# Convolution and low-rank mixer on one core: band built on chip, U laid out by matmuls, first two groups transposed on PE, x loads in held-back quarters

## The chip, the cores and the metric

The kernel runs on one core of one Trainium2 chip. The metric is the device time of one execution in microseconds (us). All but three of the timed runs were in the fast state. The three slow ones are left out of the ratios; they are still in the medians, where they move nothing by more than 0.3 us. The runs were made on different chips (the kernel before took 394.65 us in the median on the first, 392.8 to 393.2 in the later sets), so ratios are taken within one set. A ratio is the mean time of one kernel's fast runs over the mean of the other's fast runs of the same rounds, so it isn't quite the ratio of the medians quoted beside it.

Engine names are as in the profile: PE multiplies matrices, PEld loads its weights, DVE is the vector engine, ACT the scalar engine, POOL the engine that also issues the x and weight loads, SP the engine that issues the transposes and the stores. "uT" is the transposed u, "L311" a line of the kernel.

## The reference, cut to what matters

```python
# B, S, D = 8, 4224, 192;  8 heads of 24 columns, 7 taps;  rank 32;  hidden width 768
w = softmax(weight)                                   # [8 heads, 7 taps]
y[b, s] = sum_k w[head, k] * xpad[b, s + k]           # causal convolution along s, per head
h = (y^T @ U) @ V                                     # U: 4224 x 32, V: 32 x 4224
u = y + h^T
out = u + relu(u @ w_ch1) @ w_ch2                     # 192 -> 768 -> 192
```

`h` of any row needs all rows of its batch: `y^T @ U` (called tt below) sums over s. So a batch must be loaded and convolved whole before its first row of u exists.

## The kernel before

The 264 tiles of 128 rows are taken in 33 groups of eight; 33 tiles make a batch. PE does everything: the convolution as a matmul with a band matrix, tt, `h`, the first layer (W1) and the second (w2). W1 needs u with its 192 columns on the partitions, so each group's u is transposed by a DMA.

The band goes through DRAM (the softmax and some lines cut):

```python
    g_dr = tc.dram_tile([HB, H, GW], BF16, name="g_dr")
    nc.sync.dma_start(out=g_dr[:], in_=g_sb[:])
    band = cst.tile([P, H, P], BF16, name="band")
    for hf in range(2):
        nc.sync.dma_start(out=band[HB * hf : HB * hf + HB, :, :],
            in_=bass.AP(g_dr.tensor, g_dr.offset + HB, [[H * GW - 1, HB], [GW, H], [1, P]]))
```

U comes in rows of 64 bytes, straight into the layout that tt wants:

```python
    U_sb = cst.tile([P, NT, R], BF16, name="U_sb")
    nc.gpsimd.dma_start(out=U_sb[:], in_=moe_U[:].rearrange("(j p) r -> p j r", p=P))
```

The main loop loads x in whole batches. There are two x buffers, and nothing else holds POOL back: once a buffer's last convolution is multiplied, POOL issues the six loads of the next batch in a row (`...` marks a cut).

```python
    for g in range(NG + 1):
        if g + 1 < NG:
            h_group(g + 1)            # h by matmul, u = y + h on DVE
            transp(g + 1)             # DMA transpose of u, issued by SP
        for b in loadq.get(g, []):
            x_tile(b)
            for ch in XCH:
                x_load(b, *ch)        # two DMAs each, three chunks
        if g < NG:
            w1(g)                     # 36 matmuls, 12 PSUM banks, relu on ACT (8) and DVE (4)
        for b, h in convq.get(g, []):
            conv(b, h, 0, NB1, "AA")
        ...                           # w2(g-1) in four parts; tt_mm, tt_split in the middle
        for b in tts:
            tt_sum(b)                 # after the last part of w2
```

## Time and profile before

| | |
|---|---|
| time, median of three runs | 394.76 us (394.54 to 394.97) |
| span of the profiled run | 393.3 us, mean granted clock 0.953 |
| busy: PE, DVE, ACT | 84%, 60%, 48% |
| start of the first W1 | 43.3 us |
| PE waiting for uT, in six places | 32.2 us |
| group without / with two heads of convolution, undisturbed (the two differ in more than the convolution, see the last point of the account) | 8.73 / 9.20 us |

The page of the profile first: the span in 40 slices of 9.8 us, each digit the share of a slice in tenths; PEclk is the granted clock in tenths.

```profile
PE   0070599969996999969996999959999999999995
PEclk9996599999999899989999899978999999999998
DMA  9999925993599456994599456992544574546524
```

PE is idle in the first slices and dips again in five (the 9th, 13th, 18th, 22nd and 27th), each time in the second of two slices in which DMA is full. Now the waits of PE (microseconds in total, times, longest):

```profile
PE ps L311 <- DMA uT<-u_sb: 32.2, 6, 12.8
PE ps L183 <- DMA band<-g_dr: 19.9, 2, 19.3
PE ps L256 <- DVE tt_sb L233: 4.0, 8, 0.6
```

And the chain of waits (start, duration, what), followed back from the end:

```profile
...
5.40 5.85 DMA g_dr<-g_sb
...
11.95 8.22 DMA band<-g_dr
...
32.37 10.81 DMA uT<-u_sb
43.31 7.01 PE ps L311 x36
...
116.81 11.30 DMA uT<-u_sb
128.16 5.56 PE ps L311 x36
...
```

The band's trip through DRAM holds PE until 20.2 us. A transpose that has a median of 4.1 us to landing takes 10.8 and 11.3 us here, and the W1 after it is slow: 7.01 and 5.56 us instead of the 4.05 of an undisturbed group, because the clock was 0.50 when it began (43.3 to 46.7 us and 128.2 to 131.0 us). The timeline of POOL shows what had been issued just before the second of them (start, duration, engine, line, operation, count):

```profile
109.55 0.75 POOL L76 DMA_DIRECT2D x_sb<-in_x_dram  x1 [0.28 <-issue]
...
113.29 0.75 POOL L81 DMA_DIRECT2D x_sb<-in_x_dram  x1
```

These are the first and last of six loads, a whole batch in one burst; the transpose at 116.81 runs into it.

### The profile page before, as it was taken

Reading aid. Unit: us, or ns where it says so; the run is one execution under the profiler, and the core shown is the slowest. Engines: PE = TensorE matmul, PEld = TensorE weight load, DVE = VectorE, ACT = ScalarE, POOL = GpSimd, SP = SyncE. Lnnn points to the kernel's source line nnn. Section 1 sums busy time; section 2 is a strip of 40 time slices with the busy share of each in tenths; the row PEclk is TensorE's granted clock in tenths of the full one; section 3 lists DMA queues with packets and bytes.
Section 4 is the critical chain, followed back from the end, with each engine's and each line's share of the span. In section 5 each row is a group of like instructions: output and inputs, shape, how many; then the busy total and the mean of one; then the engine's idle time right before and its main releaser. Section 6 shows DMA issues by size and latency. Waiting matters only on the chain.

```text
span 393.3 us, 9471 instructions
## 1 busy us (share of the span) xinstructions
PE 330.9 (84%) x3956; PEld 221.1 (56%) x3956; DVE 236.6 (60%) x485; ACT 189.1 (48%) x410; POOL 46.2 (12%) x77
## 2 busy tenths in 40 slices
PE   0070599969996999969996999959999999999995
PEld 0060267646664577626664577626666676666674
DVE  2064176657766376647765376735766776778763
ACT  1050387526643556536643556515655664555440
POOL 8473002200040004000040003100000000000000
PEclk9996599999999899989999899978999999999998
DMA  9999925993599456994599456992544574546524
GB/s 120 179 170 188 123 44 124 205 201 93 128 148 192 112 130 118 215 176 95 131 149 170 117 136 120 202 189 63 132 110 115 130 140 113 130 122 136 148 90 153
DMA packets 130044, 54.63 MB, mean 139 GB/s; under 512 B 95248, under 2 KB 129936, under 8 KB 130000
## 3 DMA queue, kind: packets, MB, share of 16 engines
q1 hardware_dynamic: 88864, 39.41, 44.6%
q0 software_dynamic: 41136, 14.60, 33.7%
q8 instruction: 31, 0.51, 0.5%
q14 instruction: 13, 0.11, 0.1%
HBM read 29.47 MB, written 26.15 MB: 141 GB/s over the span
## 4 chain that ended last, share of the span: by engine, by line
PE 71%; DMA 22%; DVE 3%; ACT 1%; issue 0%; SPq 0%; DVEq 0%
PE ps L311 34%; PE ps L333 28%; DMA uT<-u_sb 17%; PE ps L183 5%; DMA band<-g_dr 2%; PE ps L256 2%; PE ps L210 2%; DMA g_dr<-g_sb 1%; DVE out_sb L341 1%; ACT y_sb L196 1%; DMA out_dram<-out_sb 1%; DMA w_sb<-in_weight_dram 1%; DVE tt_sb L233 1%; DVE u_sb L278 0%; DVE g_sb L142 0%
## 5 line engine op out<-in xcount | busy, mean ns | idle before, releaser
L321 ACT ACTIVATE rl_sb<-ps 128x512 bf16<-128x512 f32 x264 | 134.8, 619 | 160.9 <-PE ps L311 129.8
L311 PE MATMUL ps<-uT,W_sb 64*128 64x512 bf16 x1188 | 148.9, 398 | 32.3 <-DMA uT<-u_sb 32.2
L333 PE MATMUL ps<-W_sb,rl_sb 128*128 128x192 bf16 x1584 | 137.5, 246 | 0.0
L333 PEld LDWEIGHTS <-rl_sb 128*128 128x128 bf16 x1584 | 128.7, 98 | 12.1 <-issue 12.1
L311 PEld LDWEIGHTS <-W_sb 64*128 64x128 bf16 x1188 | 63.5, 98 | 107.8 <-issue 34.7
L341 DVE TENSOR_TENSOR out_sb<-ps,u_sb 128x384 f32<-128x384 f32 x132 | 73.5, 558 | 78.2 <-PE ps L333 77.1
L323 DVE TENSOR_SCALAR rl_sb<-ps 128x512 bf16<-128x512 f32 x132 | 88.3, 690 | 48.2 <-PE ps L311 48.1
L278 DVE TENSOR_TENSOR u_sb<-y_sb,ps 128x192 bf16<-128x192 bf16 (+1 forms) x168 | 66.3, 461 | 0.6 <-PE ps L256 0.6
L196 ACT ACTIVATE y_sb<-ps 128x384 bf16<-128x384 f32 (+3 forms) x136 | 53.5, 516 | 18.7 <-PE ps L183 18.5
L183 PE MATMUL ps<-x_sb,band 64*64 64x408 bf16 (+4 forms) x640 | 30.6, 319 | 20.0 <-DMA band<-g_dr 19.9
L183 PEld LDWEIGHTS <-band 64*64 64x64 bf16 x640 | 17.0, 116 | 34.1 <-DMA band<-g_dr 20.1
L72 POOL MEMSET x_sb<- 64x96 uint32 x8 | 1.4, 172 | 191.5 <-issue 155.9
L81 POOL DMA_DIRECT2D x_sb<-in_x_dram x24 | 18.8, 785 | 0.4
L76 POOL DMA_DIRECT2D x_sb<-in_x_dram x24 | 18.1, 754 | 1.8 <-issue 1.8
L256 PE MATMUL ps<-tt_sb,V_sb 32*128 32x192 bf16 x264 | 13.2, 246 | 4.0 <-DVE tt_sb L233 4.0
L198 DVE CAST y_sb<-ps 128x144 bf16<-128x144 f32 (+1 forms) x24 | 5.7, 297 | 17.1 <-PE ps L183 17.1
L256 PEld LDWEIGHTS <-V_sb 32*128 32x128 bf16 x264 | 4.6, 92 | 10.3 <-issue 10.3
L210 PE MATMUL ps<-y_sb,U_sb 128*32 128x192 bf16 x264 | 8.1, 252 | 0.9 <-ACT y_sb L196 0.9
L223 ACT ACTIVATE tt_hi<-ps 128x192 bf16<-128x192 f32 x8 | 2.6, 331 | 10.2 <-PE ps L210 10.2
L210 PEld LDWEIGHTS <-U_sb 128*32 128x32 bf16 x264 | 5.9, 97 | 2.5 <-issue 2.3
L224 DVE TENSOR_TENSOR tt_lo<-ps,tt_hi 128x192 bf16<-128x192 f32 x8 | 2.9, 358 | 5.4 <-ACT tt_hi L223 5.4
L233 DVE CAST tt_sb<-ps 128x192 bf16<-128x192 f32 x8 | 2.8, 348 | 0.3 <-PE ps L231 0.3
(24 smaller groups left out, 18.9 us busy)
## 6 DMA issues: line engine op xcount, KB each, us to landing
out_dram<-out_sb SPq DMA_DIRECT2D x132, 192.0 KB, 2.0
x_sb<-in_x_dram POOLq DMA_DIRECT2D x24, 288.0 KB, 8.4
x_sb<-in_x_dram POOLq DMA_DIRECT2D x8, 312.0 KB, 6.8
x_sb<-in_x_dram POOLq DMA_DIRECT2D x8, 240.0 KB, 15.2
x_sb<-in_x_dram POOLq DMA_DIRECT2D x8, 192.0 KB, 13.3
W_sb<-in_moe_w_ch_dram POOLq DMA_DIRECT2D x3, 288.0 KB, 6.0
uT<-u_sb SPq DMA_TRANSPOSE x33, 4.1
U_sb<-in_moe_U_dram POOLq DMA_DIRECT2D x1, 264.0 KB, 11.1
```

Of the source, the lines that this page charges most:

```text
L76: nc.gpsimd.dma_start(out=xt[b][0:HB, 1 + i0 : 1 + e0, :], in_=x[b, i0 * HB : e0 * HB, :].rearrange("(j p) d -> p j d", p=HB),)
L81: nc.gpsimd.dma_start(out=xt[b][HB:P, s0 : i1 + 1, :], in_=x[b, (NB0 - 1 + s0) * HB : (NB0 + i1) * HB, :].rearrange("(j p) d -> p j d", p=HB),
L183: nc.tensor.matmul(out=pp[r][HB * c : HB * c + HB, 0 : nn[r] * GS], lhsT=band[HB * r : HB * r + HB, h, HB * halo : HB * halo + HB], rhs=xt ...
L196: nc.scalar.activation(out=o, in_=i, func=ACT.Copy)
L210: nc.tensor.matmul(out=ttp[b][32 * c : 32 * c + 32, 0:D], lhsT=U_sb[:, j, :], rhs=yt[b][:, j, :], start=(ttn[b] < 4), stop=(ttn[b] + 4 >= NT),
L256: nc.tensor.matmul(out=banks[pr][:, a * D : (a + 1) * D], lhsT=V_sb[32 * q : 32 * q + 32, (j // 8) * 2 + j % 2, :], rhs=ttb[b][32 * q : 32 ...
L278: nc.vector.tensor_tensor(out=u_group(g)[:, i : i + n, :, hf, :], in0=yt[b][:, run[0] : run[0] + n, :].rearrange("p n (c k) -> p n c k", c=3),
L311: nc.tensor.matmul(out=pp[hf][:], lhsT=W1_sb[HB * hf : HB * hf + HB, c, m * P : (m + 1) * P], rhs=uTt[g][HB * hf : HB * hf + HB, :, c, :], ...
L321: nc.scalar.activation(out=rl[:, m, hf, :], in_=pp[hf][:], func=ACT.Relu)
L323: nc.vector.tensor_scalar_max(out=rl[:, m, hf, :], in0=pp[hf][:], scalar1=0.0)
L333: nc.tensor.matmul(out=cps[:, a * D : (a + 1) * D], lhsT=rlt[g][:, m, hf, (i + a) * P : (i + a + 1) * P], rhs=W2_sb[:, m, :], start=(m == ...
L341: nc.vector.tensor_tensor(out=o[:].rearrange("p n (c k) -> p n c k", c=3), in0=cps[:, 0 : 2 * D].rearrange("p (n c k) -> p n c k", n=2, c= ...
```

## The change

Its intent has two halves. The start: make the band on chip with DVE and PE, load U in wide rows and let PE lay it out, and bring the first two groups to W1 without a DMA transpose, from PE transposes of y and a directly multiplied transposed h. The main loop: load x in quarters, one quarter a group, each held back until that group's W1 has been multiplied, so that the load doesn't meet a transpose; run the convolution one slot earlier; sum tt one part of w2 earlier. The diff, cut to its core:

```diff
-    xs = ctx.enter_context(tc.tile_pool(name="xs", bufs=2))      # ys likewise 2 -> 3
+    xs = ctx.enter_context(tc.tile_pool(name="xs", bufs=3))
 ...
-    nc.gpsimd.dma_start(out=U_sb[:], in_=moe_U[:].rearrange("(j p) r -> p j r", p=P))
+    nc.gpsimd.dma_start(out=Ur[:, 0:nfull, :], in_=U4[0 : nfull * P, :].rearrange("(k p) c -> p k c", p=P))
 ...  (loads of the second x half, V, W1, W2)
+    Eq = cst.tile([P, 4, P], BF16, name="Eq")                     # selector for the layout of U
+    nc.gpsimd.memset(Eq[:], 0.0)
+    for jj in range(4):
+        nc.gpsimd.affine_select(out=Eq[32 * jj : 32 * jj + 32, :, :], ...)
 ...
+    for _ in range(20):                                           # warm-up
+        nc.tensor.matmul(out=wps[:], lhsT=zz[:, 0:P], rhs=zz[:], start=True, stop=True)
 ...  (softmax, now on 128 partitions; g_dr and its DMAs are gone)
+    for hh in range(2):
+        bp = bank()
+        for d in range(KC):
+            pr = sml.tile([P, HQ, BW], BF16, name="pr", bufs=4)
+            nc.vector.scalar_tensor_tensor(out=pr[:], in0=dif..., scalar=float(d), in1=c_sb...,
+                                           op0=ALU.is_equal, op1=ALU.mult)
+            nc.tensor.matmul(out=bp[:, 0 : HQ * BW], lhsT=ident[:], rhs=pr[:], start=(d == 0), stop=(d == KC - 1))
+        nc.scalar.activation(out=band[:, HQ * hh : HQ * hh + HQ, 0:BW], in_=bp..., func=ACT.Copy)
 ...
-    slots = [G - 5 + k // 2 for k in range(H)]
+    slots = [G - 6 + k // 2 for k in range(H)]                    # b = 2: [3]*3 + [4]*3 + [5]*2
+    for k, ch in enumerate(QCH):                                  # four quarters
+        loadq.setdefault(max(0, slots[0] - 4 + k), []).append((b, ch))
 ...
     for k, (i0, i1) in enumerate(XCH):                            # now two halves of batch 0
         for h in range(H):
             conv(0, h, i0, i1, "AD")
+        if k == 0:
+            u_layout()                                            # 16 matmuls with Eq, 4 copies
+            yT[0] = yT_part(0)                                    # 24 PE transposes of y
         tt_mm(0, ...)
-    tt_split(0); tt_sum(0); h_group(0); transp(0)
+    yT[1] = yT_part(1); tt_sum(0); hT_part(0, yT[0]); hT_part(1, yT[1])
 ...
+            last = w1(g)                                          # the W1's last matmul
+        if g == 0:
+            h_group(0); h_group(1)                                # u of the first two groups, for the output
+        for b, ch in loadq.get(g, []):
+            for r in range(2):
+                held(x_half(b, r, *ch), last)                     # load waits for it
 ...
+            if k == 2:                                            # was: after the last w2
+                for b in tts: tt_sum(b)
```

More of the change, by code (lines that the diff above doesn't have):

```diff
@@ L45 @@
     cst = ctx.enter_context(tc.tile_pool(name="cst", bufs=1))
-    xs = ctx.enter_context(tc.tile_pool(name="xs", bufs=2))
-    ys = ctx.enter_context(tc.tile_pool(name="ys", bufs=2))
+    xs = ctx.enter_context(tc.tile_pool(name="xs", bufs=3))
+    ys = ctx.enter_context(tc.tile_pool(name="ys", bufs=3))
     us = ctx.enter_context(tc.tile_pool(name="us", bufs=5))
@@ L56, in bank @@
         return psp.tile([P, 512], F32, name="ps", tag="ps")
-    w_sb = cst.tile([HB, H, KC], F32, name="w_sb")
-    nc.sync.dma_start(out=w_sb[:], in_=weight[:].partition_broadcast(HB))
+    w_sb = cst.tile([P, H, KC], F32, name="w_sb")
+    nc.sync.dma_start(out=w_sb[:], in_=weight[:].partition_broadcast(P))
     xt = [None] * B
@@ L67 @@
     NB1 = S // HB - NB0
-    XCH = [(0, 12), (12, 24), (24, NB1)]
     def x_tile(b):
@@ L72, in x_tile, with x_half @@
         nc.gpsimd.memzero(xt[b][0:HB, 0, :])
-    def x_load(b, i0, i1):
-        e0 = min(i1, NB0)
-        nc.gpsimd.dma_start(
-            out=xt[b][0:HB, 1 + i0 : 1 + e0, :],
-            in_=x[b, i0 * HB : e0 * HB, :].rearrange("(j p) d -> p j d", p=HB),
-        )
+    def x_half(b, r, i0, i1):
+        if r == 0:
+            e0 = min(i1, NB0)
+            return nc.gpsimd.dma_start(
+                out=xt[b][0:HB, 1 + i0 : 1 + e0, :],
+                in_=x[b, i0 * HB : e0 * HB, :].rearrange("(j p) d -> p j d", p=HB),
+            )
         s0 = i0 if i0 == 0 else i0 + 1
-        nc.gpsimd.dma_start(
+        return nc.gpsimd.dma_start(
             out=xt[b][HB:P, s0 : i1 + 1, :],
@@ L86, in x_load @@
         )
+    XCH = [(0, 16), (16, NB1)]
     x_tile(0)
-    x_load(0, *XCH[0])
-    x_load(0, *XCH[1])
-    U_sb = cst.tile([P, NT, R], BF16, name="U_sb")
-    nc.gpsimd.dma_start(out=U_sb[:], in_=moe_U[:].rearrange("(j p) r -> p j r", p=P))
-    x_load(0, *XCH[2])
+    for r in range(2):
+        x_half(0, r, *XCH[0])
+    HW = KC - 1
+    BW = HB + HW
+    dif = cst.tile([P, BW], F32, name="dif")
+    for r in range(2):
+        nc.gpsimd.iota(
+            dif[HB * r : HB * r + HB, :],
+            pattern=[[1, BW]],
+            base=0,
+            channel_multiplier=-1,
+            allow_small_or_imprecise_dtypes=True,
+        )
+    NUB = (NT + 3) // 4
+    Ur = cst.tile([P, NUB, 4 * R], BF16, name="Ur")
+    U4 = moe_U[:].rearrange("(n a) r -> n (a r)", a=4)
+    nfull = NT // 4
+    nc.gpsimd.dma_start(
+        out=Ur[:, 0:nfull, :], in_=U4[0 : nfull * P, :].rearrange("(k p) c -> p k c", p=P)
+    )
+    nlast = NT * 32 - nfull * P
+    nc.gpsimd.dma_start(out=Ur[0:nlast, nfull, :], in_=U4[nfull * P :, :])
+    for r in range(2):
+        x_half(0, r, *XCH[1])
     NSL = (NT + 7) // 8 * 2
     V_sb = cst.tile([P, NSL, P], BF16, name="V_sb")
+    full = NT // 8
     for q in range(4):
-        full = NT // 8
         src = moe_V[:, 0 : full * 8 * P].rearrange("r (k q t) -> r k q t", q=4, t=2 * P)
@@ L110 @@
     )
+    V0_sb = cst.tile([32, 2 * GT * P], BF16, name="V0_sb")
+    nc.gpsimd.dma_start(out=V0_sb[:], in_=moe_V[:, 0 : 2 * GT * P])
     W1_sb = cst.tile([P, 3, M4], BF16, name="W1_sb")
@@ L118 @@
     nc.gpsimd.dma_start(out=W2_sb[:], in_=moe_w_ch2[:].rearrange("(m p) d -> p m d", p=P))
-    g_sb = cst.tile([HB, H, GW], BF16, name="g_sb")
-    nc.vector.memset(g_sb[:], 0.0)
-    wm = cst.tile([HB, H], F32, name="wm")
-    nc.vector.tensor_reduce(out=wm[:], in_=w_sb[:], axis=mybir.AxisListType.X, op=ALU.max)
-    d_sb = cst.tile([HB, H, KC], F32, name="d_sb")
-    nc.vector.tensor_tensor(
-        out=d_sb[:],
-        in0=w_sb[:],
-        in1=wm[:].unsqueeze(2).to_broadcast([HB, H, KC]),
-        op=ALU.subtract,
-    )
-    e_sb = cst.tile([HB, H, KC], F32, name="e_sb")
-    nc.scalar.activation(e_sb[:], d_sb[:], ACT.Exp)
-    s_sb = cst.tile([HB, H], F32, name="s_sb")
-    nc.vector.tensor_reduce(out=s_sb[:], in_=e_sb[:], axis=mybir.AxisListType.X, op=ALU.add)
-    s2_sb = cst.tile([HB, H], F32, name="s2_sb")
-    nc.vector.tensor_scalar_add(s2_sb[:], s_sb[:], 1e-9)
-    rs_sb = cst.tile([HB, H], F32, name="rs_sb")
-    nc.vector.reciprocal(rs_sb[:], s2_sb[:])
-    for d in range(KC):
-        nc.vector.tensor_tensor(
-            out=g_sb[:, :, HB + d],
-            in0=e_sb[:, :, KC - 1 - d],
-            in1=rs_sb[:],
-            op=ALU.mult,
-        )
-    g_dr = tc.dram_tile([HB, H, GW], BF16, name="g_dr")
-    nc.sync.dma_start(out=g_dr[:], in_=g_sb[:])
-    band = cst.tile([P, H, P], BF16, name="band")
-    for hf in range(2):
-        nc.sync.dma_start(
-            out=band[HB * hf : HB * hf + HB, :, :],
-            in_=bass.AP(g_dr.tensor, g_dr.offset + HB, [[H * GW - 1, HB], [GW, H], [1, P]]),
+    Eq = cst.tile([P, 4, P], BF16, name="Eq")
+    nc.gpsimd.memset(Eq[:], 0.0)
+    for jj in range(4):
+        nc.gpsimd.affine_select(
+            out=Eq[32 * jj : 32 * jj + 32, :, :],
+            in_=Eq[32 * jj : 32 * jj + 32, :, :],
+            compare_op=ALU.not_equal,
+            fill=1.0,
+            base=0,
+            pattern=[[-1, 4], [1, P]],
+            channel_multiplier=-4,
         )
@@ L169 @@
         )
+    zz = cst.tile([P, 512], BF16, name="zz")
+    nc.vector.memzero(zz[:])
+    ident = cst.tile([P, P], BF16, name="ident")
+    wps = bank()
+    for _ in range(20):
+        nc.tensor.matmul(out=wps[:], lhsT=zz[:, 0:P], rhs=zz[:], start=True, stop=True)
+    band = cst.tile([P, H, P], BF16, name="band")
+    nc.vector.memzero(band[:])
+    e_sb = cst.tile([P, H, KC], F32, name="e_sb")
+    mx_sb = cst.tile([P, H], F32, name="mx_sb")
+    nc.vector.tensor_reduce(out=mx_sb[:], in_=w_sb[:], axis=mybir.AxisListType.X, op=ALU.max)
@@ new lines @@
+    d_sb = cst.tile([P, H, KC], F32, name="d_sb")
+    nc.vector.tensor_tensor(
+        out=d_sb[:],
+        in0=w_sb[:],
+        in1=mx_sb[:].unsqueeze(2).to_broadcast([P, H, KC]),
+        op=ALU.subtract,
+    )
+    nc.scalar.activation(e_sb[:], d_sb[:], ACT.Exp)
+    nc.vector.memzero(ident[:])
+    for r in range(2):
+        nc.vector.tensor_scalar(
+            out=ident[HB * r : HB * r + HB, HB * r : HB * r + HB],
+            in0=dif[HB * r : HB * r + HB, 0:HB],
+            scalar1=0.0,
+            scalar2=None,
+            op0=ALU.is_equal,
+        )
@@ new lines @@
+    s_sb = cst.tile([P, H], F32, name="s_sb")
+    nc.vector.tensor_reduce(out=s_sb[:], in_=e_sb[:], axis=mybir.AxisListType.X, op=ALU.add)
+    s2_sb = cst.tile([P, H], F32, name="s2_sb")
+    nc.vector.tensor_scalar_add(s2_sb[:], s_sb[:], 1e-9)
+    rs_sb = cst.tile([P, H], F32, name="rs_sb")
+    nc.vector.reciprocal(rs_sb[:], s2_sb[:])
+    c_sb = cst.tile([P, H, KC], F32, name="c_sb")
+    nc.vector.tensor_tensor(
+        out=c_sb[:],
+        in0=e_sb[:],
+        in1=rs_sb[:].unsqueeze(2).to_broadcast([P, H, KC]),
+        op=ALU.mult,
+    )
@@ new lines @@
+    HQ = H // 2
+    for hh in range(2):
+        bp = bank()
+        for d in range(KC):
+            pr = sml.tile([P, HQ, BW], BF16, name="pr", bufs=4)
+            nc.vector.scalar_tensor_tensor(
+                out=pr[:],
+                in0=dif[:].unsqueeze(1).to_broadcast([P, HQ, BW]),
+                scalar=float(d),
+                in1=c_sb[:, HQ * hh : HQ * hh + HQ, KC - 1 - d : KC - d].to_broadcast(
+                    [P, HQ, BW]
+                ),
+                op0=ALU.is_equal,
+                op1=ALU.mult,
+            )
+            nc.tensor.matmul(
+                out=bp[:, 0 : HQ * BW],
+                lhsT=ident[:],
+                rhs=pr[:],
+                start=(d == 0),
+                stop=(d == KC - 1),
+            )
+        nc.scalar.activation(
+            out=band[:, HQ * hh : HQ * hh + HQ, 0:BW],
+            in_=bp[:, 0 : HQ * BW].rearrange("p (h t) -> p h t", h=HQ),
+            func=ACT.Copy,
+        )
@@ new lines, with u_layout @@
+    U_sb = cst.tile([P, NUB, 4, R], BF16, name="U_sb")
+    def u_layout():
+        up = [bank() for _ in range(4)]
+        nb = [nfull + (1 if 32 * jj < nlast else 0) for jj in range(4)]
+        for a in range(4):
+            for jj in range(4):
+                nc.tensor.matmul(
+                    out=up[jj][:, 0 : nb[jj] * R],
+                    lhsT=Eq[32 * jj : 32 * jj + 32, a, :],
+                    rhs=Ur[32 * jj : 32 * jj + 32, 0 : nb[jj], a * R : (a + 1) * R],
+                    start=(a == 0),
+                    stop=(a == 3),
+                    tile_position=(32 * jj, 0),
+                )
+        for jj in range(4):
+            o = U_sb[:, 0 : nb[jj], jj, :]
+            i = up[jj][:, 0 : nb[jj] * R].rearrange("p (k r) -> p k r", r=R)
+            if jj % 2 == 0:
+                nc.scalar.activation(out=o, in_=i, func=ACT.Copy)
+            else:
+                nc.vector.tensor_copy(out=o, in_=i)
@@ L198, in conv @@
                 nc.vector.tensor_copy(out=o, in_=i)
-    ttp = [None] * B
-    ttb = [None] * B
-    ttn = [0] * B
+    ttb = [[] for _ in range(B)]
     def tt_mm(b, js):
-        if ttp[b] is None:
-            ttp[b] = bank()
-        for j in js:
-            c = ttn[b] % 4
+        p = bank()
+        for n, j in enumerate(js):
+            c = n % 4
             nc.tensor.matmul(
-                out=ttp[b][32 * c : 32 * c + 32, 0:D],
-                lhsT=U_sb[:, j, :],
+                out=p[32 * c : 32 * c + 32, 0:D],
+                lhsT=U_sb[:, j // 4, j % 4, :],
                 rhs=yt[b][:, j, :],
-                start=(ttn[b] < 4),
-                stop=(ttn[b] + 4 >= NT),
+                start=(n < 4),
+                stop=(n + 4 >= len(js)),
                 tile_position=(0, 32 * c),
             )
-            ttn[b] += 1
-    def tt_split(b):
         hi = sml.tile([P, D], BF16, name="tt_hi")
         lo = sml.tile([P, D], BF16, name="tt_lo")
-        nc.scalar.activation(out=hi[:], in_=ttp[b][:, 0:D], func=ACT.Copy)
-        nc.vector.tensor_tensor(out=lo[:], in0=ttp[b][:, 0:D], in1=hi[:], op=ALU.subtract)
-        ttb[b] = (hi, lo)
+        nc.scalar.activation(out=hi[:], in_=p[:, 0:D], func=ACT.Copy)
+        nc.vector.tensor_tensor(out=lo[:], in0=p[:, 0:D], in1=hi[:], op=ALU.subtract)
+        ttb[b] += [hi, lo]
     def tt_sum(b):
-        hi, lo = ttb[b]
         p = bank()
-        nc.tensor.matmul(out=p[:, 0:D], lhsT=R4[:], rhs=hi[:], start=True, stop=False)
-        nc.tensor.matmul(out=p[:, 0:D], lhsT=R4[:], rhs=lo[:], start=False, stop=True)
+        for n, part in enumerate(ttb[b]):
+            nc.tensor.matmul(
+                out=p[:, 0:D],
+                lhsT=R4[:],
+                rhs=part[:],
+                start=(n == 0),
+                stop=(n + 1 == len(ttb[b])),
+            )
         t = sml.tile([P, D], BF16, name="tt_sb")
@@ L300, in transp, with yT_part, hT_part @@
         )
+    def yT_part(g):
+        yT = uts.tile([P, 4, 3, P], BF16, name="yT", bufs=2)
+        tp = [psp.tile([P, 1024], BF16, name="ps", tag="ps") for _ in range(2)]
+        for n in range(12):
+            i, c = n // 3, n % 3
+            for hf in range(2):
+                nc.tensor.matmul(
+                    out=tp[n // 6][HB * hf : HB * hf + HB, (n % 6) * P : (n % 6 + 1) * P],
+                    lhsT=yt[0][:, GT * g + 4 * hf + i, HB * c : HB * c + HB],
+                    rhs=ident[:],
+                    start=True,
+                    stop=True,
+                    is_transpose=True,
+                    tile_position=(0, HB * hf),
+                )
+        for k in range(2):
+            o = yT[:, 2 * k : 2 * k + 2, :, :].rearrange("p i c t -> p (i c t)")
+            if k == 0:
+                nc.scalar.activation(out=o, in_=tp[k][:, 0 : 6 * P], func=ACT.Copy)
+            else:
+                nc.vector.tensor_copy(out=o, in_=tp[k][:, 0 : 6 * P])
+        return yT
+    def hT_part(g, yT):
+        uTt[g] = uts.tile([P, 4, 3, P], BF16, name="uT")
+        for c in range(3):
+            p = bank()
+            for hf in range(2):
+                nc.tensor.matmul(
+                    out=p[HB * hf : HB * hf + HB, :],
+                    lhsT=ttb[0][0:32, HB * c : HB * c + HB],
+                    rhs=V0_sb[:, (2 * g + hf) * 4 * P : (2 * g + hf + 1) * 4 * P],
+                    start=True,
+                    stop=True,
+                    tile_position=(0, HB * hf),
+                )
+            nc.vector.tensor_tensor(
+                out=uTt[g][:, :, c, :],
+                in0=yT[:, :, c, :],
+                in1=p[:].rearrange("p (i t) -> p i t", i=4),
+                op=ALU.add,
+            )
     RELU = ["AA", "AD", "AA", "AD", "AD", "AD"]
@@ L310, in w1 @@
                 for hf in range(2):
-                    nc.tensor.matmul(
+                    last = nc.tensor.matmul(
                         out=pp[hf][:],
@@ L323, in w1 @@
                     nc.vector.tensor_scalar_max(out=rl[:, m, hf, :], in0=pp[hf][:], scalar1=0.0)
+        return last
     out_t = out.rearrange("b s d -> (b s) d").rearrange("(t p) d -> p t d", p=P)
@@ L351 @@
     ttq = {}
+    loadq = {}
+    QCH = [(0, 8), (8, 16), (16, 24), (24, NB1)]
     for b in range(1, B):
         G = (b * NT) // GT
-        slots = [1] * 4 + [2] * 4 if b == 1 else [G - 5 + k // 2 for k in range(H)]
+        if b == 1:
+            slots = [1] * 4 + [2] * 4
+        elif b == 2:
+            slots = [3] * 3 + [4] * 3 + [5] * 2
+        else:
+            slots = [G - 6 + k // 2 for k in range(H)]
         for h, s in zip(range(H), slots):
@@ L357, with held @@
         ttq.setdefault(G - 2, []).append(b)
-    loadq = {}
-    for b in range(2, B):
-        G = (b * NT) // GT
-        loadq.setdefault(max(1, G - 10), []).append(b)
-    for (i0, i1) in XCH:
+        if b > 1:
+            for k, ch in enumerate(QCH):
+                loadq.setdefault(max(0, slots[0] - 4 + k), []).append((b, ch))
+    def held(ins, after):
+        tc.add_manual_dep(
+            ins.ins,
+            after.ins.name,
+            mybir.DependencyInfo(mybir.DependencyClass.Sync, mybir.DependencyReason.DATA),
+            reason="load held back",
+        )
+    yT = [None, None]
+    for k, (i0, i1) in enumerate(XCH):
         for h in range(H):
             conv(0, h, i0, i1, "AD")
-        tt_mm(0, list(range(i0 // 2, min(i1, NB0) // 2)) + list(range((NB0 + i0) // 2, (NB0 + i1) // 2)))
-    tt_split(0)
+        if k == 0:
+            u_layout()
+            yT[0] = yT_part(0)
+        tt_mm(
+            0,
+            list(range(i0 // 2, min(i1, NB0) // 2))
+            + list(range((NB0 + i0) // 2, (NB0 + i1) // 2)),
+        )
+    yT[1] = yT_part(1)
     tt_sum(0)
-    h_group(0)
-    transp(0)
+    hT_part(0, yT[0])
+    hT_part(1, yT[1])
     x_tile(1)
-    for ch in XCH:
-        x_load(1, *ch)
+    for ch in QCH:
+        for r in range(2):
+            x_half(1, r, *ch)
     for g in range(NG + 1):
-        if g + 1 < NG:
+        if g + 1 < NG and g > 0:
             h_group(g + 1)
             transp(g + 1)
-        for b in loadq.get(g, []):
-            x_tile(b)
-            for ch in XCH:
-                x_load(b, *ch)
         if g < NG:
-            w1(g)
+            last = w1(g)
+        if g == 0:
+            h_group(0)
+            h_group(1)
+        for b, ch in loadq.get(g, []):
+            if ch[0] == 0:
+                x_tile(b)
+            for r in range(2):
+                held(x_half(b, r, *ch), last)
         for b, h in convq.get(g, []):
@@ L389 @@
         tts = ttq.get(g, [])
-        if g > 0:
-            w2(g - 1, 0)
-            w2(g - 1, 1)
-        for b in tts:
-            tt_mm(b, range(NT))
-            tt_split(b)
-        if g > 0:
-            w2(g - 1, 2)
-            w2(g - 1, 3)
-        for b in tts:
-            tt_sum(b)
+        for k in range(4):
+            if g > 0:
+                w2(g - 1, k)
+            if k == 1:
+                for b in tts:
+                    tt_mm(b, range(NT))
+            if k == 2:
+                for b in tts:
+                    tt_sum(b)
 _INS = ['x', 'weight', 'moe_U', 'moe_V', 'moe_w_ch1', 'moe_w_ch2']
```

## The prediction

> **What bounds the kernel now.** The span is 393.3 us. From 295.0 us on the chain of waits shows PE back to back, 8.73 us for a group without convolution (346.30 to 355.03), 9.2 with two heads, clock 1.0: bound by PE. 31 such groups, 56 heads at 0.405 us, seven U sums at 0.9, the lone first W1 (4.4) and the 16.7 us from the last W1's start to the end give about 321 us after the first W1 starts, at 43.3 us: 364. The other 29 us are lost in the middle.
>
> - PE's waits: 32.2 us for the transposed u, 12.8 at the start and 19.4 in five later places. There the chain shows 10.5 to 12.3 us for a transpose (median 4.1), and the timeline six x loads issued in a row just before (109.5 to 114.0 us), DMA share above 1.2 until 130. The Trainium skill, "DMA: Bandwidth & Descriptors", section "Issuing engines are not separate DMA queues", says all queues share 16 engines and interleave; this trace agrees.
> - After each such wait the clock falls to 0.50 and W1 takes 5.5 to 7.0 us instead of 4.05 ("TensorE: Matmul & The Clock Gate", Part 1, says idling halves the clock; the windows show it): about 10 us in all.
> - 4.0 us waiting for tt_sb, eight times 0.5.
>
> Start: PE waits until 19.3 us for the band (g_dr 5.85 us, band 8.2 us by DMA), although the last x chunk landed by 17.9 (waits of POOL). Then 8 us of convolution, tt and h, then the 10.8 us first transpose.
>
> **What the change does, costed.**
> - Band on chip: after the softmax (5.3 us) 14 vector operations of 280 elements at about 0.37 us (estimate from the 0.36 us of a 192-wide subtract): ready near 11.5 us, like the first x half. PE can start 8 us earlier.
> - U layout: 16 matmuls and four evictions, 1.5 to 2 us. But its selector Eq stands on POOL behind all weight loads, and POOL stalls until the load issued eight earlier has landed (as at 9.9, 12.3, 15.8 now). I expect Eq at 19 to 22 us, and PE, in order, idle from 14 until then. This returns much of the band's gain.
> - After Eq: layout, 24 transposes, tt, second convolution half, tt, 24 transposes, tt_sum, h transposed: about 12.5 us. First W1 near 33.5 us, warm, instead of 43.3 cold: 10 plus 3 us gained.
> - Given back: six adds of 128x512 (0.69 us) and twelve u additions (0.47) meet the relus on DVE in groups 0 and 1: 15 us of DVE against 10 of PE; PE stalls 3 to 4 us.
> - Held quarters: a transpose is issued 2 us into a group and lands 4 us later; a quarter of x starts only after W1, at 4.4 us. Nearly all 19.4 us of waits and 7 us of cold W1 go; 1 to 2 us remain.
> - tt_sum one w2 earlier: 3 to 4 us gained.
>
> **Sum.** 33.5 + 321 + 3.5 + residue 0 to 2 = 358 span; times lie 1.5 above it: 359 us. Range 351 to 368. Faster by over 2%: 0.95; within 2%: 0.04; slower: 0.01.
>
> **What would show it.** First W1 at 31 to 36 us; PE's wait for uT below 3 us; clock 1.0 from 40 us; u_layout preceded by a wait for Eq; 8.73 us groups unchanged; W1 of group 0 or 1 stretched by DVE.
>
> **What would make it wrong.** Eq much later or earlier; quarters landing on the transposes all the same, since 28 of 33 groups carry one; the transpose of group 2 held up by x(1) and x(2), leaving a cold stretch near 45 to 55 us.

## The result, and the profile after

The kernel after takes 354.05 us (353.87 to 354.23, four runs); before, 394.65 us. The ratio is 0.8984, with a 95% interval of 0.8945 to 0.9023: 10% faster. The span is 352.1 us, the mean clock 0.981, PE is busy 96% of it. The page's slices, now 8.8 us each:

```profile
PE   8589899999999999999999999999999999999995
PEclk9869899999999999999999999999999999999999
DMA  9979989976989899878969897899445454555535
```

From the sixth slice on PE has no dip left, and the load traffic is spread evenly instead of coming in bursts. The waits of PE:

```profile
PE ps L256 <- POOL Eq L151: 4.6, 4, 3.8
PE ps L356 <- DVE u_sb L378: 0.7, 3, 0.2
```

No wait for uT by DMA is left in the list; a transpose has a median of 3.7 and a maximum of 5.2 us to landing, against 4.1 and 12.7. A new wait stands first, for Eq. The chain of waits in the start:

```profile
...
15.73 0.89 POOL W_sb L145
...
20.03 1.03 PE ps L256 x10
...
30.96 2.36 PE ps L455 x20
33.35 1.99 DVE rl_sb L467 x3
35.34 2.79 DVE u_sb L378 x6
38.17 5.73 PE ps L455 x35
...
```

The first W1 runs at 30.0 us (its main part at 30.96) instead of 43.3. The second takes 5.73 us, as slow as one after a transpose wait: between 34.5 and 38.2 us PE was busy for 2.4 of 3.7 us, since it could only put in its h matmuls as DVE freed banks one by one. The busy time by stretch shows the clock there (stretch, PE, PEld, DVE, ACT and POOL busy with counts, clock, DMA share, GB/s):

```profile
36.00:38.00 2.00, 1.18 (x9) 0.47 (x8) 2.00 (x5) 0.00 (x0) 1.70 (x3) 1.00 0.93 100
40.00:42.00 2.00, 2.00 (x12) 0.89 (x10) 1.50 (x3) 1.12 (x3) 0.00 (x0) 0.54 1.23 140
```

Last, one quarter and the transposes around it, in the timelines of POOL and SP:

```profile
105.26 0.69 POOL L76 DMA_DIRECT2D x_sb<-in_x_dram  x1 [8.96 <-PE ps L455]
105.94 0.70 POOL L81 DMA_DIRECT2D x_sb<-in_x_dram  x1
```

```profile
103.12 1.43 SPq L397 DMA_TRANSPOSE uT<-u_sb  x1
...
112.32 2.71 SPq L397 DMA_TRANSPOSE uT<-u_sb  x1
```

POOL had waited 8.96 us for W1 (L455). The two loads of the quarter go out 2 us after one transpose and 6 us before the next, land 3.7 to 4.1 us later, and so fit between.

The undisturbed groups are what they were: in the chain W1, w2 and h of a group without convolution take 8.73 us (306.06 to 314.79).

### The profile page after: what moved, and what is told of

It reads as the page before. It is cut to its first block, busy times and chain, and to the rows that moved or that the text cites. A ratio compares the mean times of both kernels' runs of the same rounds, so it can differ in the third digit from the quotient of the medians.

```text
span 352.1 us, 9621 instructions
## 1 busy us (share of the span) xinstructions
PE 338.9 (96%) x4004; PEld 228.7 (65%) x4004; DVE 246.1 (70%) x500; ACT 191.0 (54%) x409; POOL 56.5 (16%) x98
## 4 chain that ended last, share of the span: by engine, by line
PE 90%; DVE 4%; DMA 3%; POOL 2%; issue 1%; ACT 0%; POOLq 0%
PE ps L455 39%; PE ps L478 38%; PE ps L284 6%; DMA x_sb<-in_x_dram 3%; PE ps L356 2%; PE ps L308 2%; DVE u_sb L378 1%; DVE y_sb L299 1%; PE ps L409 1%; POOL Eq L151 1%; DVE rl_sb L467 1%; DVE uT L439 1%; POOL x_sb L76 0%; PE ps L325 0%; DVE out_sb L486 0%
## 5 line engine op out<-in xcount | busy, mean ns | idle before, releaser
L465 ACT ACTIVATE rl_sb<-ps 128x512 bf16<-128x512 f32 x264 | 133.3, 623 | 121.5 <-issue 66.2
L455 PE MATMUL ps<-uT,W_sb 64*128 64x512 bf16 x1188 | 143.6, 380 | 0.8 <-DVE uT L439 0.2
L478 PEld LDWEIGHTS <-rl_sb 128*128 128x128 bf16 x1584 | 128.8, 98 | 12.2 <-issue 12.2
L455 PEld LDWEIGHTS <-W_sb 64*128 64x128 bf16 x1188 | 64.3, 95 | 69.2 <-issue 14.0
L297 ACT ACTIVATE y_sb<-ps 128x384 bf16<-128x384 f32 (+2 forms) x128 | 52.6, 528 | 0.3
L76 POOL DMA_DIRECT2D x_sb<-in_x_dram x30 | 21.2, 705 | 178.7 <-PE ps L455 163.2
L284 PE MATMUL ps<-x_sb,band 64*64 64x408 bf16 (+3 forms) x576 | 29.5, 335 | 0.0
L81 POOL DMA_DIRECT2D x_sb<-in_x_dram x30 | 22.1, 736 | 0.0
L180 PE MATMUL ps<-zz 128*128 128x512 bf16 x20 | 6.0, 471 | 1.2 <-DVE zz L176 1.2
L256 PE MATMUL ps<-Ur,Eq 32*128 32x256 bf16 (+1 forms) x16 | 2.2, 410 | 4.6 <-POOL Eq L151 4.6
L299 DVE CAST y_sb<-ps 128x192 bf16<-128x192 f32 (+1 forms) x16 | 5.1, 366 | 1.0 <-PE ps L284 1.0
```

The costliest lines, as they stand in the source:

```text
L76: return nc.gpsimd.dma_start(out=xt[b][0:HB, 1 + i0 : 1 + e0, :], in_=x[b, i0 * HB : e0 * HB, :].rearrange("(j p) d -> p j d", p=HB),)
L81: return nc.gpsimd.dma_start(out=xt[b][HB:P, s0 : i1 + 1, :], in_=x[b, (NB0 - 1 + s0) * HB : (NB0 + i1) * HB, :].rearrange("(j p) d -> p j ...
L284: nc.tensor.matmul(out=pp[r][HB * c : HB * c + HB, 0 : nn[r] * GS], lhsT=band[HB * r : HB * r + HB, h, HB * halo : HB * halo + HB], rhs=xt ...
L297: nc.scalar.activation(out=o, in_=i, func=ACT.Copy)
L455: last = nc.tensor.matmul(out=pp[hf][:], lhsT=W1_sb[HB * hf : HB * hf + HB, c, m * P : (m + 1) * P], rhs=uTt[g][HB * hf : HB * hf + HB, :, ...
L465: nc.scalar.activation(out=rl[:, m, hf, :], in_=pp[hf][:], func=ACT.Relu)
```

## The experiments

Twelve variants ran, all correct. "First W1" is its first matmul in the trace; "uT wait" is PE's total wait for DMA transposes.

| run | built on | time, us | ratio to before (95%) | first W1, us | uT wait, us |
|---|---|---|---|---|---|
| before | | 394.65 | 1 | 43.3 | 32.2 |
| after | | 354.05 | 0.8984 (0.8945 to 0.9023) | 30.0 | 0 |
| loads_only | before | 366.64 | 0.9324 (0.929 to 0.9359) | 36.3 | 9.9 |
| old_loads | after | 381.90 | 0.971 (0.9669 to 0.9752) | 30.1 | 18.2 |
| no_hold | after | 381.34 | 0.9713 (0.9646 to 0.978) | 30.3 | 16.7 |
| whole_held | after | 379.22 | 0.9645 (0.9602 to 0.9689) | 30.0 | 20.1 |
| eq_early | after | 349.58 | 0.8891 (0.8857 to 0.8925) | 26.1 | 0 |
| u_direct | after | 347.57 | 0.8855 (0.8825 to 0.8886) | 23.3 | 0 |
| band_dram | after | 355.81 | 0.9065 (0.9033 to 0.9097) | 31.7 | 0 |
| dma_first | after | 363.32 | 0.9237 (0.9193 to 0.928) | 38.8 | 12.3 |
| u_direct_band_dram | u_direct | 357.44 | 0.9088 (0.9036 to 0.9141) | 32.6 | 0 |
| u_direct_spread | u_direct | 351.03 | 0.8923 (0.8878 to 0.8968) | 23.3 | 2.8 |
| sum_late | after | 357.25 | 0.908 (0.9035 to 0.9124) | 30.1 | 0 |
| conv_back | after | 353.61 | 0.8999 (0.8952 to 0.9045) | 30.0 | 0 |

The kernel after was timed in an earlier set than its variants, so a difference of two medians in this table carries the 1 to 2 us by which sets differ; conv_back, which does the same work, came within 0.5 us of it in the last set. All the larger differences below also hold between the ratios, but their sizes shift: taken from the ratios, the gain of eq_early is 3.7 us (4.5 from the medians), that of u_direct 5.1 (6.5), the loss of band_dram 3.2 (1.8) and that of sum_late 3.8 (3.2). The spans of the profiled runs agree with the medians for u_direct (345.4 against 352.1) and band_dram (353.9). No run undoes the warm-up matmuls, the third y buffer or the two halves of batch 0 by themselves, and none tries the held quarters with two x buffers.

The first two questions are how the 40 us divide between the loads and the start, and what it is about the loads that helps: their size, their time, or the third buffer.

### loads_only: the loads of the change, nothing else

```diff
 (kernel before)
-    xs ... bufs=2
+    xs ... bufs=3
-        loadq.setdefault(max(1, G - 10), []).append(b)
+        for k, ch in enumerate(QCH):
+            loadq.setdefault(max(0, G - 9 + k), []).append((b, ch))
 ...
+            last = w1(g)
+        for b, ch in loadq.get(g, []):
+            for ld in x_load(b, *ch): held(ld, last)
```

> The kernel before, with only its x loads changed: four quarters per batch, one a group, each held until the first layer (W1) of its group has been multiplied. Theory: the five later waits for the transposed u (19.4 us) and the slow first layers after them (about 7 us) came from whole-batch loads, so both go, the start stays at 43.3 us, and the time is 366 to 370 us. Rival: the start-up work is most of the gain, and the later waits only move; then the time stays above 380 us.

Measured: 366.64 us. The time is inside the expected interval, but the way there isn't the expected one. The chain of waits:

```profile
32.09 4.05 DMA uT<-u_sb
36.28 4.37 PE ps L312 x24
...
44.53 11.50 DMA uT<-u_sb
56.08 4.01 PE ps L312 x19
```

The start did not stay at 43.3 us. The first transpose took 4.05 us instead of 10.81, although the loads of V, the weights and x(1) are there as before. What is missing is x(2): in the kernel before, its buffer became free when the last convolution of x(0) was multiplied, and its six loads went out just before the transpose.

```profile
27.85 0.17 POOL L72 MEMSET x_sb<- 64x96 uint32 x1 [1.80 <-PE ps L183]
...
32.07 0.72 POOL L81 DMA_DIRECT2D x_sb<-in_x_dram  x1
```

So about 7 us of the wait at the start were the same collision as the later ones. In return this run loses time at the transpose of group 2 (11.50 us): the first three quarters of x(2) were issued close together, from 42.2 to 48.0 us, in groups 0 and 1. PE waits 3.85 us there and its W1 is slow again (5.75 us), about 5.5 us in all.

### old_loads: everything but the loads

```diff
 (kernel after)
-    xs ... bufs=3
+    xs ... bufs=2
-            for k, ch in enumerate(QCH): loadq.setdefault(max(0, slots[0] - 4 + k), []).append((b, ch))
+            loadq.setdefault(max(1, G - 10), []).append(b)
-                held(x_half(b, r, *ch), last)            # after w1
+            for ch in [(0, 12), (12, 24), (24, NB1)]: ... x_half(b, r, *ch)     # before w1, not held
```

> The kernel after, with the loads of before put back (whole batches, not held, two x buffers). Theory: the start-up gain (13 us) and the early tt_sum (3 us) stay, the waits for transposes come back: 374 to 384 us, with some 4 us of waiting at each of about five places. Rival: with the start gone the transposes no longer collide; then under 360 us.

Measured: 381.90 us, PE waits 18.2 us for uT in five places, as before. The rival falls. The two runs agree on the division: the loads are worth 26 to 28 us (392.8 to 366.6 from one side, 381.9 to 354.05 from the other), the rest of the change 11 to 13 us. That they agree so well is partly luck: the 26 of loads_only include the 7 us at the start, which the change cures a second time by its new start, less the 5.5 us that this run loses anew at group 2.

### no_hold: quarters, but not held back

```diff
 (kernel after)
-                held(x_half(b, r, *ch), last)
+                x_half(b, r, *ch)
```

> The kernel after, with the quarters no longer held back; they start as soon as a buffer is free. Theory: it is the release after W1 that keeps a load off the next transpose; without it the eight pieces of a batch run in one burst and PE waits for transposes again: 370 to 384 us. Rival: cutting the loads in quarters (or the third buffer) is enough; then 354 to 357 us.

Measured: 381.34 us. POOL, held by nothing but a free buffer, issues all eight pieces of a batch in a row; here the last of them, and the piece of the chain of waits that follows:

```profile
101.01 0.80 POOL L81 DMA_DIRECT2D x_sb<-in_x_dram  x1
```

```profile
102.39 11.35 DMA uT<-u_sb
113.79 5.37 PE ps L455 x36
```

Quarters and a third buffer alone give back nothing of the 27 us. The rival falls.

### whole_held: held back, but a whole batch at once

```diff
 (kernel after)
-                loadq.setdefault(max(0, slots[0] - 4 + k), []).append((b, ch))
+                loadq.setdefault(max(0, slots[0] - 4), []).append((b, ch))
```

> The kernel after, with all four quarters of a batch released at one point, after the W1 of the first of the four groups. Theory: a batch takes 10 to 12 us, longer than the 4.7 us left of the group, so it runs into the next transpose and costs 3 to 5 us at each of six batches: 366 to 378 us. Rival: the point of release is what matters, not the size; then 354 to 357 us.

Measured: 379.22 us, a little above the expected interval; PE waits 20.1 us in six places. Held release alone gives next to nothing either (2.7 us less than old_loads, and the intervals of the two ratios overlap): the burst starts after W1 and is still running when the next transpose is issued. Of the kernels tried, only those with both, a load small enough and released at the right time, are free of the collision in the main loop.

### eq_early: the selector built before the weight loads

Now the start. PE's only large wait after the change is for Eq, which POOL builds behind the weight loads:

```profile
16.66 0.52 POOL L149 MEMSET Eq<- 128x512 bf16 x1
17.26 2.72 POOL L151 TENSOR_SCALAR_AFFINE_SELECT Eq<-Eq 32x512 bf16<-32x512 bf16 x4
```

```diff
 (kernel after: the block that builds Eq moved up)
     for r in range(2):
         x_half(0, r, *XCH[1])
+    Eq = ...; nc.gpsimd.memset(...); 4 x nc.gpsimd.affine_select(...)
     (loads of V, V0, W1, W2)
-    Eq = ...
```

> The kernel after, with the selector Eq built on POOL before the loads of V and the weights are issued, instead of behind them. Theory: PE's wait of 4.6 us for Eq goes, and the cold stretch from 14 to 22 us with it; the second x half landed by 15.1 us; the first W1 moves from 30.0 to 25 to 27 us and the time from 354.0 to 349 to 351 us. Rival: the weight loads, now issued 3 us later, or the second x half become the next wait; then under 2 us are gained.

Measured: 349.58 us, first W1 at 26.1 us, no wait for Eq: 4.5 us gained, as expected. A cost that nobody had expected shows up beside it. The operations that build the band, read by tile (shortest, median and longest in ns), first in the kernel after, then in this run:

```profile
L225 DVE SCALAR_TENSOR_TENSOR pr<-dif,c_sb x14: 440/442/451, 5.8 to 10.6; 128x280 bf16<-128x280 f32 x14
```

```profile
L225 DVE SCALAR_TENSOR_TENSOR pr<-dif,c_sb x14: 435/438/885, 7.3 to 13.7; 128x280 bf16<-128x280 f32 x14
```

While POOL makes its selections (7.4 to 10.6 us), a DVE operation takes up to 885 ns instead of 442, and a selection 734 instead of 630. The convolution starts at 14.5 instead of 11.4 us. About half of these 3 us is this slowing (the fourteen operations take 6.9 us from first to last instead of 5.2). The other half is a later beginning (7.25 instead of 5.81): DVE's wait for the convolution weights ended 0.8 us later in this profile (4.59 against 3.79), although nothing before that load was changed, and the small vector operations after it took 0.6 us longer. The Trainium skill states this in "GPSIMD Engine Reference", section "Specifications": POOL shares its SBUF interfaces with DVE, with contention for DVE instructions that have two SBUF inputs. `scalar_tensor_tensor` has two here, and this trace agrees.

### u_direct: U loaded as before, no layout

```diff
 (kernel after)
-    Ur ... two loads in rows of 256 bytes;  Eq ...;  u_layout()
+    U_sb = cst.tile([P, NT, R], BF16, name="U_sb")
+    nc.gpsimd.dma_start(out=U_sb[:], in_=moe_U[:].rearrange("(j p) r -> p j r", p=P))
```

> The kernel after, with U loaded straight into its layout as before (4224 packets of 64 bytes), without Eq and the layout matmuls. Theory: the old U load took about 3.6 us of the queue against about 1 us now, so the second x half lands near 18 us, where PE now waits for Eq until 20.0 and lays U out until 21; so the layout by matmuls gains nothing: 352 to 355 us. Rival: the old load also holds the whole queue up and the layout is worth its 2 us and more: over 356 us.

Measured: 347.57 us, 6.5 us faster than the kernel after and below the expected interval; the fastest kernel. The layout of U by matmuls doesn't merely gain nothing, it costs 6.5 us. Most of this is the wait for the selector: eq_early, which has the layout without that wait, stands only 2.0 us above u_direct in the same set. The first convolution half ends at 15.0 us and the transposes of y follow at once, where the kernel after does them at 21.0. The expectation erred in what the 64-byte load costs: the wait of POOL for the last part of the second x half ends at 16.27 us against 15.11, so it delays x by 1.2 us (it had been reckoned at 2.6, and x at 18 us):

```profile
15.11 0.63 POOL L140 DMA_DIRECT2D W_sb<-in_moe_w_ch_dram  x1 [1.75 <-DMA x_sb<-in_x_dram]
```

```profile
16.27 0.63 POOL L133 DMA_DIRECT2D W_sb<-in_moe_w_ch_dram  x1 [1.77 <-DMA x_sb<-in_x_dram]
```

In the kernel before, U had seemed to take 3.6 us of the queue (12.2 to 15.8). The band's DMAs ran in that time, but they are not the reason: u_direct_band_dram below has both, and there the wait ends at 16.33 us. More likely the 3.6 us were shared with the last two x loads, which landed 0.9 and 2.0 us after U (16.7 and 17.9 us); no run shows it.

### band_dram: the band through DRAM again

```diff
 (kernel after)
-    (14 x scalar_tensor_tensor and matmul with ident, 2 copies)
+    (g_sb on 64 partitions, g_dr, two band DMAs, as in the kernel before)
```

> The kernel after, with the band built through DRAM as before. Theory: the band comes near 19 us instead of 11.5; PE is in order, so the first convolution half (2.8 us) then stands after the wait instead of inside it, and since Eq holds PE until 20.0 anyway, only some 3 to 4 us of the 8 are lost, with the colder clock: 356.5 to 359 us. Rival: the full 8 us are lost: 361 us or more.

Measured: 355.81 us, first W1 at 31.7 us: 1.8 us lost, less than either theory had. PE waits for the band until 20.15 us, but Eq would have held it until 20.0 in any case, and the convolution then runs into a U layout that needs no wait.

### u_direct_band_dram: the same, with the selector out of the way

```diff
 (u_direct)
-    (band on chip)
+    (band through DRAM)
```

> The run u_direct (347.6 us) with the band through DRAM as well. Theory: in band_dram the loss was only 1.8 us because PE would have waited for Eq until 20.0 us anyway; with Eq gone nothing hides the band, which comes at about 20 us instead of 12.3, so about 8 us are lost: 354.5 to 357 us. Rival: the band through DRAM is cheap by itself; then 348 to 350.5 us.

Measured: 357.44 us, first W1 at 32.6 instead of 23.3 us. Without Eq in the way the band on chip is worth 9.9 us, with it 1.8. The two parts of the change stand in the way of each other: one takes a wait of PE away, the other puts a new one in the same place. Its runs spread wider than the others (355.27 to 359.14 us), so the 9.9 is uncertain by some 2 us; the time is also slightly above the expected interval.

### dma_first: the first two groups transposed by DMA

```diff
 (kernel after)
-            yT[0] = yT_part(0)
-    yT[1] = yT_part(1); tt_sum(0); hT_part(0, yT[0]); hT_part(1, yT[1])
+    tt_sum(0); h_group(0); transp(0)
-        if g + 1 < NG and g > 0:
+        if g + 1 < NG:
```

> The kernel after, with the first two groups transposed by DMA as before. Theory: the x(1) load runs beside the first transpose as it did before, so it takes 7 to 11 us, PE idles that long and goes cold, while the transposes on PE (2.4 us) and the second set of adds fall away: 361 to 366 us. Rival: the first transpose costs its 4 us of landing only: 355 to 358 us.

Measured: 363.32 us. The transpose of group 0 takes 7.86 us beside the load of x(1), and the one of group 2 takes 10.11:

```profile
30.84 7.86 DMA uT<-u_sb
...
47.55 10.11 DMA uT<-u_sb
```

The transposes on PE are worth 9.3 us here, the largest part of the new start. A rival to them was not tried: to release x(1) later and keep the DMA transposes. In loads_only, where x(1) was issued by 25.4 us, the first transpose at 32.09 took only 4.05 us.

### u_direct_spread: fewer u additions between the first two W1

```diff
 (u_direct)
-        if g == 0:
-            h_group(0)
-            h_group(1)
+        if g in (1, 2):
+            h_group(g - 1)
```

> The run u_direct with the u additions of groups 0 and 1 moved behind the W1 of groups 1 and 2, so that no more than eight of them stand in one group. Theory: PE's stall on banks between the first two W1 (27.9 to 31.0 us, where three groups of matmuls alone take about 1 us) and the cold second W1 (6.2 instead of 4.1 us) come from twelve additions in a row on DVE; both go: 343 to 345 us. Rival: the earlier transpose of group 2 then falls on the loads of x(1) and x(2) and PE waits for it: 347 us or more.

Measured: 351.03 us, 3.5 us slower than u_direct (2.7 from the ratios, whose intervals touch): the rival was right, although the theory's mechanism was there too. The stall between the first two W1 is gone and the second W1 is warm; but the transpose of group 2, issued at 30.49 instead of 34.22 us, now stands in the loads of x(1) and x(2), and lands only after 12.0 us:

```profile
28.23 4.10 PE L411 MATMUL ps<-uT,W_sb 64*128 64x512 bf16 x36
...
42.54 5.49 PE L411 MATMUL ps<-uT,W_sb 64*128 64x512 bf16 x36 [2.77 <-DMA uT<-u_sb]
```

The stall on DVE had been holding the transpose out of the burst. Whether a later release of the first quarters of x(2) would let both gains stand has not been tried.

### sum_late and conv_back: the two small parts

```diff
 (sum_late: kernel after)                          (conv_back: kernel after)
-            if k == 2: tt_sum                     -   slots = [3]*3 + [4]*3 + [5]*2   and  G - 6 + k // 2
+        (after the last w2): tt_sum               +   slots = G - 5 + k // 2           for b = 2 to 7
```

> The kernel after, with tt_sum behind the last w2 of its group, as before. Theory: PE waits 0.5 us for tt_sb at each of seven batches: 357 to 358 us. Rival: under 355 us.

Measured: 357.25 us, 3.2 us more, and the waits of PE show why:

```profile
PE ps L356 <- DVE tt_sb L333: 3.5, 7, 0.6
```

> The kernel after, with the convolutions of batches 2 to 7 one group later, as before (the loads follow them). Theory: the PE work is the same and y is needed only in the group with tt, where PE then waits 0.1 to 0.2 us for ACT; the time stays within 1 us of 354.0. Rival: the last convolution delays tt_mm and the chain behind it, 356 us or more.

Measured: 353.61 us against 354.05, and the intervals of the ratios overlap: the earlier convolution slot moves nothing that can be seen.

## Why the prediction was right or wrong, point by point

- **The time: right.** 359 us were predicted with a range of 351 to 368; 354.05 were measured, 5 us lower.
- **What bound the kernel: right.** PE in the steady state, and losses in the middle. The 8.73 us group is unchanged, the waits for uT are gone, and old_loads, no_hold and whole_held bring them back (18.2, 16.7 and 20.1 us) with the slow W1 behind them. One detail was too general: the W1 is not slow after each wait. In the kernel before PE had idled 3.31 us before the W1 at 85.02 us, which ran at clock 1.00 (4.06 us), and 3.16 us before the one at 171.51, which began at 0.61 (5.75 us). The prediction put the main loop at 26 us of waits and cold W1, less 1 to 2; the loads measure 26 to 28 us.
- **The division between the halves: wrong in one term.** The prediction counted all of the first transpose's delay to the start and its own cure. loads_only shows that about 7 us of it (first W1 at 36.3 instead of 43.3) were x(2) being loaded early into a freed buffer, so the loads alone would have cured that as well. The time of the change isn't touched by this, since both cures are in it.
- **Eq: right, and its price was right in kind.** "This returns much of the band's gain": Eq's first part came at 17.9 and its last at 20.0 us (19 to 22 predicted), PE waited 4.6 us, and the band on chip is worth 1.8 us with it and 9.9 us without. That the layout of U as a whole, with this wait, is a loss of 6.5 us was not foreseen; it was costed at 1.5 to 2 us of work and a wait, but never set against the 64-byte load that it replaces.
- **The first W1: too late by 3.5 us.** 33.5 predicted (31 to 36 named as the test), 30.0 measured. The main term is the stretch after Eq: 12.5 us reckoned, 10.0 measured (20.0 to 30.0); the last 1 us is Eq itself, reckoned at about 21 and there at 20.0. Layout, transposes and tt overlap with the work of ACT and DVE: the second batch of 24 transposes takes 0.86 us, the second convolution half 2.5.
- **DVE in the first groups: right, and somewhat worse.** 3 to 4 us of stall were predicted. From the first matmul of the first W1 to the end of the second pass 13.9 us (30.0 to 43.9), against 2 x 4.4 without a stall: 5.1 us lost. The prediction did not see that the stall also makes PE cold (clock 0.54 at 40 to 42 us), so its test "clock 1.0 from 40 us on" failed there; u_direct_spread shows that with the lump gone the second W1 takes 4.10 us.
- **tt_sum: right.** 3 to 4 us predicted, 3.2 measured.
- **The undisturbed 321 us after the first W1: some 4 us too much.** Measured are 322.1 us (30.0 to 352.1), and 5.1 of them are the stall, so about 317 are left. The convolution was sized right: two heads take 0.81 us, 0.405 each. Too large was the group to which they were added: 8.73 us is a group of batch 7, in which W1 takes 4.39 us. It takes that long wherever the u made beside it is of an odd batch, and 4.04 where it is of an even one (between the two where a group has tiles of both); so a group with two heads takes 9.55 us in the first case and 9.20 in the second. The trace shows a wait that only the first kind has. First a group of an odd batch, then one of an even batch:

```profile
90.12 4.46 PE L455 MATMUL ps<-uT,W_sb 64*128 64x512 bf16 x36
90.42 2.06 DVE L378 TENSOR_TENSOR u_sb<-y_sb,ps 128x192 bf16<-128x192 bf16 x6
91.81 2.27 PEld L455 LDWEIGHTS <-W_sb 64*128 64x128 bf16 x23 [0.51 <-DVE u_sb L378]
```

```profile
119.25 4.11 PE L455 MATMUL ps<-uT,W_sb 64*128 64x512 bf16 x36
119.55 1.94 DVE L378 TENSOR_TENSOR u_sb<-y_sb,ps 128x384 bf16<-128x384 bf16 x4
```

A batch has 33 tiles, so in an odd batch the eight tiles of a group cut across the pairs in which h is made: six additions and five banks instead of four and four. The load of W1's 14th weights then waits for one of the additions. Sixteen groups have this wait and twelve run at 4.04 us; twelve times 0.35 are the 4 us. No run was made to test it.

Of the span 358 us were predicted and 352.1 measured. These 5.9 us are the two mis-sized terms (3.5 and 4), less the 1.6 us by which the stall on DVE was taken too small (3.5 in the sum, 5.1 measured).

## What to carry to other kernels

A prefetch that is held back only by a free buffer starts when the buffer happens to be free, and its burst can fall on a short transfer that the bottleneck engine waits for; cut the load to what fits between two such transfers and tie its release to a point in the schedule, for here neither half of that measure gained more than 3 us alone. Undo every part of a change that touches one wait both alone and with its neighbour: the band on chip was worth 1.8 us with the U layout beside it and 9.9 without, and the layout, with the wait for its selector, cost 6.5. A stall that is taken away can release something else too early, as the group 2 transpose shows.

## What the Trainium skill lacked or had wrong

- "DMA: Bandwidth & Descriptors": the page says that all queues run on the same 16 engines and interleave, but gives no figure for a DMA transpose beside a bulk load. Here it takes 3.7 us to landing in the median when kept apart (5.2 at most), and up to 12.7 us beside a whole-batch load (4224 rows of 384 bytes as bf16).
- "DMA: Bandwidth & Descriptors", section "Why small descriptors are slow (HBM only)": the section explains why short descriptors are slow, which speaks for wider rows, but has no figure for a load of this kind. Here U in 4224 rows of 64 bytes (as bf16) instead of 1056 of 256 delayed the x load behind it by only 1.2 us (16.27 against 15.11; between 14.9 and 15.6 in the profiles of the other kernels with the wide load).
- "TensorE: Matmul & The Clock Gate", Part 4: the page gives about 275 to 390 ns for one PE transpose of 128x128. One of 128x64 here takes 278 ns in the median, which is near the lower figure. What the page lacks is how fast they follow each other: 24 of them, placed in two column halves, took 0.86 us at full clock and 1.49 us at half clock, back to back: 36 and 62 ns each.
- The same page, Part 1, names long idle gaps, and also frequent short ones between groups of matmuls, as what halves the clock, but gives no busy share for the short ones. Here PE was busy 1.18 of 2 us at 36 to 38 us, in pieces with gaps of some 0.23 us, and the clock was 0.54 at 40 to 42 us.
- "GPSIMD Engine Reference": the contention with two-input DVE instructions has no figure there. Here the DVE operation took up to 885 ns instead of 442, and the POOL operation 734 instead of 630.
